# Attention and a channel MLP on one core: reordering the first batch's loads, casts and row work

## The chip, the core and the metric

The kernel runs on one core of a Trainium2 chip. The metric is device time in microseconds of one execution. Before the change it is 813.15 us, the median of five runs (812.42 to 814.14).

The engines named below: TensorE (PE in the profile, its weight loads PEld) multiplies matrices and writes to PSUM banks; VectorE (DVE) and ScalarE (ACT) do elementwise work and move PSUM results to SBUF; GpSimd (POOL) does some casts and issues the transfers that convert f32 to bf16 on the way; SyncE (SP) issues other transfers. Each engine runs its own instructions strictly in the order in which the program gives them, and waits at each for what it needs from the others.

## What is computed

Eight batches of 384 positions. First grouped attention: 16 query heads on 4 key and value heads, 64 wide. Its heads side by side are x, 384 x 1024. Then an MLP block in which tokens and channels are mixed in turn:

```python
scores = scale * np.matmul(q, k.transpose(0, 1, 3, 2))
attn = softmax(scores)                       # with the maximum taken off
x = np.matmul(attn, v)                       # heads side by side: B x 384 x 1024
a1 = alpha1 * x + beta1
tok = np.einsum('ts,bsd->btd', w_tok, a1)    # w_tok: 384 x 384
u = x + lam * tok
a2 = alpha2 * u + beta2
ch = np.maximum(a2 @ w_ch1, 0.0) @ w_ch2     # 1024 -> 4096 -> 1024
out = u + lam * ch
```

## The kernel before

**Stages.** `side(b)` lists the attention and the token mixing of batch b as small units; `main(b)` is the channel MLP of batch b, the bulk of TensorE's work. For b of 1 and more the units of `side(b)` are spread between the matmuls of `main(b - 1)`. Batch 0 has no MLP in front of it, so `side(0)` runs alone, and this is the stage that the change touches. Nothing reorders instructions: the order of the calls is the order on each engine.

**The order of the first batch.** There are 18 steps `scores(i)`, each with an exponential on ScalarE. After step i come the units that the table `at` lists for i (lines 375 to 382). The score tiles take turns in two PSUM buffers, so scores(i) needs the exponential of step i - 2. `av(p)` multiplies the weights of head pair p with v; its norm on VectorE is a reciprocal, a multiplication (into x) and a multiplication by a row (lines 242, 243, 247). `tok(p)` mixes tokens, and VectorE adds the result to x (line 266). `ut` transposes the result and ScalarE scales it (line 278). `k_transpose` and `q_transpose` turn k and q on TensorE and copy the result to kT and qT (lines 179, 190). The tags "tp" and "av" are one PSUM bank each and are shared by all transposes and row products, so each user of a tag waits until the last reader of the user before it is done.

**The rows alpha and beta.** The rows lie in a scratch of 32 partitions, `rows_f`, one block of 128 columns for each (0 alpha1, 1 beta1, 2 alpha2, 3 lam, 4 beta2). `scale_rows(i)` multiplies a row by lam (line 521). `split` cuts f32 rows into three bf16 parts, with a cast and a multiply and subtract (lines 529, 530), twice, and a last cast (533); on the way it uses the scratch `rows_t`. `spread` multiplies them out to all partitions on TensorE and copies the result to `vecs` (lines 325, 327), in two halves, `lower` and `upper`. `rows_r` makes the row R of w_tok's column sums times beta (lines 307 to 317); `fill_h` makes its counterpart H from beta's split (line 537). `tok` multiplies both (line 263). The scratches are all pieces of hT, which is free until the MLP starts:

```python
rows_f = hTf[:32, 9216:10496].bitcast(f32)
rows_t = hTf[:32, 10496:11520].bitcast(f32)
t = hTf[:32, 10496:10496 + S]          # in rows_r
```

**Loads.** SyncE's queue loads k (two tiles of two heads) and the rows; ScalarE's queue q's first group and v; GpSimd's queue the other three q groups (`load_q4`), w_tok, and the weights W1 (`load_w1`, chunks of 256 columns in a ring of five buffers), then the next batch's q and v and W2. v is cast to bf16 by GpSimd (line 545). `place_k` casts a k tile and doubles it, two instructions a call; the call `place_k(0, 1)`, heads 2 and 3, has both on GpSimd (line 101).

Of the kernel before, what the change touches and what calls it, by code (L numbers as in the profile page):

```python
# [12 lines left out]
def kernel(  # L13
# [21 lines left out]
    nc = tc.nc  # L35
# [7 lines left out]
    B, Hq, S, D = q.shape  # L43
# [23 lines left out]
    vt = [const.tile([P, NST, Hkv, D1], bf, tag=f"v{i}", name=f"v{i}") for i in range(2)]  # L67
# [25 lines left out]
    def place_k(b, i, hs=(0, 1)):  # L93
        if b not in k2s:
            k2s[b] = sb.tile([P, NST, Hkv, 2, D], bf, tag="k2", name="k2", bufs=1)
        copies = [nc.gpsimd.tensor_copy] * 2
        if b == 1 or b == 0 == i:
            copies = (nc.vector.tensor_copy, nc.vector.tensor_copy if i else nc.scalar.copy)
        lo, hi = hs[0], hs[-1] + 1
        for a in range(2):  # L100
            copies[a](out=k2s[b][:, :, 2 * i + lo:2 * i + hi, a, :], in_=ks[b][i][:, lo:hi].rearrange("p h st d -> p st h d"))
# [22 lines left out]
    def load_w1(n):  # L124
        if n < B * NCH:
            t = sb.tile([P, NDT, CW * P], bf, tag="w1", name="w1", bufs=RING)
            c = n % NCH
            nc.gpsimd.dma_start(out=t, in_=w1src[:, :, c * CW * P:(c + 1) * CW * P])  # L128
            w1_tiles[n] = t
# [28 lines left out]
    def side(b):  # L158
# [145 lines left out]
        def rows_r(tag):  # L304
            ps = psum.tile([P, 512], f32, tag=tag, name="r", bufs=1)
            for st in range(NST):
                nc.tensor.matmul(out=ps[:32, :S], lhsT=ones, rhs=wtokT[:, st, :], start=(st == 0),
                                 stop=(st == NST - 1))
            turned = ps[:, S:S + 2 * NP].rearrange("p (i n) -> p i n", i=2)
            for i, c in enumerate((2, 4)):  # L310
                nc.tensor.matmul(out=turned[:, i], lhsT=rows_f[:NP, c * P:(c + 1) * P], rhs=ident_f[:NP, :NP],
                                 is_transpose=True, start=True, stop=True, skip_group_check=True)
            t = hTf[:32, 10496:10496 + S]
            nc.vector.tensor_copy(out=t, in_=ps[:32, :S])
            nc.vector.scalar_tensor_tensor(out=R[:32], in0=t, scalar=masks[2], in1=ps[:32, :S], op0=MUL, op1=ADD)
            nc.vector.tensor_copy(out=al2T, in_=turned[:, 0])
            nc.vector.tensor_copy(out=a2T[:, :, S:S + 1], in_=turned[:, 1, :, None])
# [51 lines left out]
        lower, upper = range(NP // 2), range(NP // 2, NP)  # L369
        def av(p):  # L370
# [4 lines left out]
        at = {0: [(warmup, 3)], 1: [(k_transpose, 1, 1), (scale_rows, 0), (split, 0, 1, 0)],  # L375
              2: [(q_transpose, 2, 2, "av"), (split, 0, 1, 1)], 3: [(warmup, 1)],
              4: [(spread, lower, (0, 1), "tp"), (wtok_transpose, 0, "av")], 5: [(av, 0), (wtok_transpose, 1, "tp")],
              6: [(wtok_transpose, 2, "av"), (scale_rows, 1), (split, 1, 2), (k_transpose, 2)],
              7: [(av, 1), (q_transpose, 4, 2, "av")], 8: [(rows_r, "tp"), (fill_h, 0)],
              9: [(av, 2), (spread, upper, (0, 1), "av")], 10: [(q_transpose, 6, 2), (tok, 0)],  # L380
              11: [(av, 3)], 12: [(tok, 1), (ut, 0)], 13: [(av, 4), (tok, 2)], 14: [(ut, 1), (fill_h, 4), (tok, 3)],
              15: [(av, 5), (ut, 2)], 16: [(tok, 4), (ut, 3)], 17: [(av, 6), (tok, 5)]}
        for i in range(18):
# [70 lines left out]
    with tc.manual_schedule(engines=order):  # L454

        def warmup(n):
            warm = psum.tile([P, 512], f32, tag="mm", name="warm", bufs=2)
            for _ in range(n):
# [12 lines left out]
        qst, vst = (stage[:, i:i + Hkv * NST * D].rearrange("p (h st d) -> p h st d", h=Hkv, st=NST)  # L471
                    for i in (0, Hkv * NST * D))
# [28 lines left out]
        def load_q4(g):  # L501
            nc.gpsimd.dma_start(out=qgs[g], in_=q[0, g * G:(g + 1) * G].rearrange("h (p st) d -> p h st d", st=NST))
# [36 lines left out]
                                    in1=sel4[:, p:p + 4, None].to_broadcast([32, 4, P]), op=MUL)  # L539

        nc.gpsimd.dma_start(out=wtok_in, in_=moe_w_tok.rearrange("(p tt) s -> p tt s", tt=NST))
        load_q4(2)
        load_q4(3)
        place_k(0, 0, (0,))
        nc.gpsimd.tensor_copy(out=vt[0][:, :, :, :D], in_=vst.rearrange("p h st d -> p st h d"))
        load_w1(0)
        load_w1(1)
        place_k(0, 1)
        for c in range(2, RING):
            load_w1(c)  # L550

# [4 lines left out]
        for f in side(0):  # L556
            f()
        place_k(1, 0)
        place_k(1, 1)
        for b in range(B):  # L560
            us = side(b + 1) if b + 1 < B else []
            half = False
            done, t, loaded, flipped = 0, 0, b + 2 >= B, b + 2 >= B
            lead, span = (0.04, 0.82) if b == 0 else (0, 0.95)
            if not loaded:
                load_k(b + 2)
            for dt in main(b):
                t += dt
                half = not half
                if late and half:  # L570
                    late.pop(0)()
                if done < len(us) and done * t_all * span < len(us) * (t - t_all * lead):
                    us[done]()
                    done += 1
                if not loaded and t > t_all * 0.55:
                    loaded = True
                    place_k(b + 2, 0)
                    place_k(b + 2, 1)
                    load_q(b + 2)
                    load_v(b + 2)  # L580
                if not flipped and t > t_all * 0.85:
                    flipped = True
                    flip_k(b + 2)
                    flip_q(b + 2)
            while done < len(us):
                us[done]()
                done += 1
# [30 lines left out]
```

## Time and profile before

| | |
|---|---|
| median of five runs | 813.15 us |
| the profiled execution, its own time | 812.7 us |
| its span | 810.8 us |
| granted TensorE clock | 0.999 |
| TensorE busy | 795.9 us, 98% |
| VectorE, ScalarE, GpSimd busy | 345.2, 225.2, 176.1 us |
| first batch before its MLP | 0 to about 41 us |

The span runs from the first to the last instruction; the profiled execution took 1.9 us more than its span. In the timelines a row gives the start, the duration, the engine, the line, the operation, output<-input, the shape and the count of instructions; the bracket is the idle time of the engine ahead of it and what ended it. The chain of waits is the work that ended last, followed back. DMA rows on POOL give the time of issuing; landing comes later. In the first 41 us TensorE waits 1.32 us for the rows' split, 0.97 us for the copies of w_tok, 0.9 us for a copy of q, 0.63 us for an addition to x and 0.51 us for a copy of k, apart from its wait at the start.

### The profile page before, as it was taken

The numbers are of one execution on the slowest core, as the hardware profiler recorded it, in microseconds if no ns is written. First come the engines' busy times: TensorE is split into PE (matmuls) and PEld (weight loads), VectorE is DVE, ScalarE is ACT, GpSimd is POOL, SyncE is SP. The second block draws the span as 40 slices with busy tenths as digits, with TensorE's granted clock in tenths as the row PEclk, the third lists the DMA queues.
The fourth block names the chain that finished last, engine by engine and source line by source line (L and its number), as shares of the span: only waits on it lengthen the run. The fifth ranks groups of instructions, "written<-read, shape, count | busy, mean of one in ns | idle before, by whom it ended". The sixth has DMA issues, their size and how long they took to land.

```text
span 810.8 us, 14106 instructions
## 1 busy us (share of the span) xinstructions
PE 795.9 (98%) x6076; PEld 450.0 (56%) x6129; DVE 345.2 (43%) x671; ACT 225.2 (28%) x309; POOL 176.1 (22%) x230
## 2 busy tenths in 40 slices
PE   7999999999999999999999999999999999999997
PEld 4766555665556655566455654556555565556545
DVE  7745543244433444344452445434444344432122
ACT  5654311332113311233103331034211432102100
POOL 6135330234003230133202250022500321003000
PEclk9999999999999999999999999999999999999999
DMA  9999999999179992799848997499935999129611
GB/s 188 197 201 200 204 206 182 170 159 182 36 142 181 176 139 67 134 181 165 114 100 133 174 179 87 107 145 171 180 67 110 149 177 123 39 66 178 93 40 40
DMA packets 232494, 113.16 MB, mean 140 GB/s; under 512 B 81384, under 2 KB 226288, under 8 KB 232432
## 3 DMA queue, kind: packets, MB, share of 16 engines
q0 software_dynamic: 169152, 83.28, 83.2%
q1 hardware_dynamic: 62208, 28.20, 14.8%
q8 instruction: 48, 0.79, 0.4%
q10 hardware_dynamic: 1072, 0.79, 0.3%
q14 instruction: 14, 0.11, 0.0%
HBM read 170.53 MB, written 12.58 MB: 226 GB/s over the span
## 4 chain that ended last, share of the span: by engine, by line
PE 94%; DVE 4%; issue 1%; ACT 0%; DVEq 0%
PE ch L441 41%; PE h L407 39%; PE av L237 4%; PE sc L202 4%; PE tok L259 4%; DVE x L243 1%; DVE hT L417 1%; PE h L152 1%; DVE a1f L250 0%; DVE a L252 0%; PE warm L459 0%; PE ut L276 0%; DVE hT L530 0%; PE tp L188 0%; DVE hT L529 0%
## 5 line engine op out<-in xcount | busy, mean ns | idle before, releaser
L407 PE MATMUL h<-a2T,w 128*128 128x384 bf16 (+1 forms) x2016 | 349.5, 326 | 0.9 <-DVE hT L417 0.3
L441 PE MATMUL ch<-w,hT 128*128 128x512 bf16 (+2 forms) x1547 | 345.3, 370 | 4.3 <-issue 1.0
L407 PEld LDWEIGHTS <-w 128*128 128x128 bf16 x2016 | 189.4, 98 | 125.5 <-issue 8.7
L441 PEld LDWEIGHTS <-hT 128*128 128x128 bf16 x1600 | 146.3, 98 | 154.2 <-issue 5.8
L128 POOL DMA_DIRECT2D w<-in_moe_w_ch_dram x128 | 112.1, 876 | 538.9 <-PE h L407 495.3
L211 ACT ACTIVATE es<-sc 128x1024 bf16<-128x1024 f32 x126 | 123.3, 1021 | 289.5 <-PE sc L202 289.5
L417 DVE TENSOR_SCALAR hT<-h,bias 128x384 bf16<-128x384 f32 x128 | 79.1, 618 | 187.0 <-PE h L407 186.4
L415 ACT ACTIVATE hT<-h,bias 128x384 bf16<-128x384 f32 x128 | 74.2, 580 | 202.8 <-PE h L407 202.3
L446 DVE TENSOR_TENSOR o<-ch,vecs 128x512 f32<-128x512 f32 (+2 forms) x50 | 33.4, 667 | 91.1 <-PE ch L441 91.1
L266 DVE TENSOR_TENSOR x<-tok,x 128x384 f32<-128x384 f32 x64 | 35.5, 555 | 80.5 <-PE tok L259 78.2
L237 PEld LDWEIGHTS <-es 128*128 128x128 bf16 x1008 | 45.8, 97 | 20.5
L237 PE MATMUL av<-v,es 128*128 128x65 bf16 x1008 | 49.0, 193 | 0.0
L202 PE MATMUL sc<-qT,kT 64*128 64x384 bf16 (+2 forms) x576 | 45.7, 273 | 1.2 <-DVE qT L190 0.9
L259 PEld LDWEIGHTS <-wtokT 128*128 128x128 bf16 x576 | 37.9, 98 | 12.8 <-issue 1.0
L242 DVE RECIPROCAL rinv<-av 128x6 f32<-128x6 f32 x64 | 12.3, 192 | 70.5 <-PE av L237 70.4
L259 PE MATMUL tok<-a,wtokT 128*128 128x128 bf16 x504 | 37.3, 219 | 0.0
L243 DVE TENSOR_TENSOR x<-av,rinv 128x384 f32<-128x384 f32 x64 | 35.7, 558 | 2.2
L202 PEld LDWEIGHTS <-kT 64*128 64x128 bf16 x576 | 19.9, 94 | 29.2 <-issue 23.9
L447 DVE TENSOR_TENSOR o<-o,x 128x512 f32<-128x512 f32 (+2 forms) x50 | 33.6, 671 | 1.7
L270 DVE TENSOR_TENSOR a<-x,vecs 128x384 bf16<-128x384 f32 x56 | 31.8, 567 | 1.9
L252 DVE TENSOR_TENSOR a<-a1f,vecs 128x384 bf16<-128x384 f32 x56 | 31.2, 558 | 2.2
L250 DVE TENSOR_TENSOR a1f<-x,vecs 128x384 f32<-128x384 f32 x56 | 31.2, 558 | 1.9
(76 smaller groups left out, 195.1 us busy)
## 6 DMA issues: line engine op xcount, KB each, us to landing
w<-in_moe_w_ch_dram POOLq DMA_DIRECT2D x138, 512.0 KB, 7.9
out_dram<-o SPq DMA_DIRECT2D x47, 256.0 KB, 2.1
q_raw<-in_q_dram POOLq DMA_DIRECT2D x28, 192.0 KB, 7.0
kst<-in_k_dram SPq DMA_DIRECT2D x16, 192.0 KB, 4.0
w<-in_moe_w_ch_dram POOLq DMA_DIRECT2D x1, 2048.0 KB, 15.3
v<-in_v_dram POOLq DMA_DIRECT2D x21, 64.0 KB, 6.9
w<-in_moe_w_ch_dram POOLq DMA_DIRECT2D x4, 256.0 KB, 8.8
a2T<-a SPq DMA_TRANSPOSE x54, 2.3
```

The source lines that it names most:

```text
L128: nc.gpsimd.dma_start(out=t, in_=w1src[:, :, c * CW * P:(c + 1) * CW * P])
L202: nc.tensor.matmul(out=sc[:, hh, k % 4:k % 4 + n], lhsT=kT[r, sk, 2 * p // G, :], rhs=qT[r, p, st:st + n, :], start=True, stop=True)
L211: nc.scalar.activation(out=e, in_=sc, func=EXP, scale=scale_qk)
L237: nc.tensor.matmul(out=av[:, hh, sq, :], lhsT=ess[k // 4][:, m % 2, k % 4, :], rhs=vb[:, sk, hk, :], start=(sk == 0), stop=(sk == NST - 1))
L243: nc.vector.tensor_tensor(out=x[:, :, cols(p)].rearrange("p st (h d) -> p h st d", h=2), in0=av[:, :, :, :D], in1=rinv.to_broadcast([P, 2, ...
L259: nc.tensor.matmul(out=ps[:, tt, :], lhsT=wtokT[:, st, tt * P:(tt + 1) * P], rhs=a1s[p][:, st, :], start=(st == 0), stop=(st == NST - 1 an ...
L266: nc.vector.tensor_tensor(out=u, in0=ps, in1=u, op=ADD)
L407: nc.tensor.matmul(out=ps[:, :n], lhsT=w1[:, dt, j * P:(j + 1) * P], rhs=a2T[:, dt, :n], start=(dt == 0), stop=(dt == NDT - 1))
L415: nc.scalar.activation(out=hT[:, nt, :], in_=ps[:, :S], func=RELU, bias=c1)
L417: nc.vector.tensor_scalar(out=hT[:, nt, :], in0=ps[:, :S], scalar1=c1, scalar2=0.0, op0=ADD, op1=mybir.AluOpType.max)
L441: nc.tensor.matmul(out=ps[:, lo:hi], lhsT=hT[:, nt, ms * P:(ms + 1) * P], rhs=w2[:, nt, dw * 512 + lo:dw * 512 + hi], start=(nt == 0), sto ...
L447: nc.vector.tensor_tensor(out=o[:, lo:hi], in0=o[:, lo:hi], in1=x[:, ms, c], op=ADD)
```

## The change

Four things in the first batch. On GpSimd, the loads of q groups 2 and 3 are issued behind v's cast rather than ahead of it, and `place_k(0, 1)` stands ahead of W1's first two chunks rather than behind them. In the table `at`, the scaling and the split of beta move from step 6, ahead of the copy of k, to step 7, behind the norm of pair 1 and the copy of q. The cast at the start of `rows_r` (line 314) and the copy of the upper half of alpha's spread (line 327) go from VectorE to ScalarE. TensorE's order of instructions is the same.

```diff
-            nc.vector.tensor_copy(out=t, in_=ps[:32, :S])
+            nc.scalar.copy(out=t, in_=ps[:32, :S])
             nc.vector.scalar_tensor_tensor(out=R[:32], in0=t, scalar=masks[2], in1=ps[:32, :S], op0=MUL, op1=ADD)
...
-              6: [(wtok_transpose, 2, "av"), (scale_rows, 1), (split, 1, 2), (k_transpose, 2)],
-              7: [(av, 1), (q_transpose, 4, 2, "av")], 8: [(rows_r, "tp"), (fill_h, 0)],
-              9: [(av, 2), (spread, upper, (0, 1), "av")], 10: [(q_transpose, 6, 2), (tok, 0)],
+              6: [(wtok_transpose, 2, "av"), (k_transpose, 2)],
+              7: [(av, 1), (q_transpose, 4, 2, "av"), (scale_rows, 1), (split, 1, 2)], 8: [(rows_r, "tp"), (fill_h, 0)],
+              9: [(av, 2), (spread, upper, (0, 1), "av", "ACT")], 10: [(q_transpose, 6, 2), (tok, 0)],
...
         nc.gpsimd.dma_start(out=wtok_in, in_=moe_w_tok.rearrange("(p tt) s -> p tt s", tt=NST))
+        place_k(0, 0, (0,))
+        nc.gpsimd.tensor_copy(out=vt[0][:, :, :, :D], in_=vst.rearrange("p h st d -> p st h d"))
         load_q4(2)
         load_q4(3)
-        place_k(0, 0, (0,))
-        nc.gpsimd.tensor_copy(out=vt[0][:, :, :, :D], in_=vst.rearrange("p h st d -> p st h d"))
+        place_k(0, 1)
         load_w1(0)
         load_w1(1)
-        place_k(0, 1)
         for c in range(2, RING):
             load_w1(c)
```

`place_k(0, 0, (0,))` runs on VectorE and ScalarE and keeps its place there.

## The prediction

> **What bounds the kernel now.** I read the page first, then the chain of waits, then the timeline of each engine up to 45 us, because every line of the diff acts on the first batch.
>
> ```profile
> span 810.8 us, 14106 instructions
> PE 795.9 (98%) x6076; PEld 450.0 (56%) x6129; DVE 345.2 (43%) x671; ACT 225.2 (28%) x309; POOL 176.1 (22%) x230
> PE 94%; DVE 4%; issue 1%; ACT 0%; DVEq 0%
> ```
>
> TensorE carries 94% of the chain. The 4% on VectorE is where a change can act, and most of it lies between 8 and 24 us. TensorE's instructions there, with what ended each wait:
>
> ```profile
> 11.79 0.38 PE L325 MATMUL vec<-hT,stage 128*128 128x128 bf16 x4 [1.32 <-DVE hT L533]
> ...
> 15.05 0.49 PE L177 MATMUL tp<-ident,k 128*128 128x128 bf16 x6 [0.97 <-DVE wtokT L300]
> 15.81 0.72 PE L237 MATMUL av<-v,hT 128*128 128x65 bf16 x18
> 16.36 0.50 PE L188 MATMUL tp<-ident,qg 128*128 128x128 bf16 x6
> ...
> 17.69 0.65 PE L307 MATMUL r<-wtokT,stage 128*32 128x384 bf16 x3 [0.51 <-DVE kT L179]
> 19.45 0.39 PE L202 MATMUL sc<-qT,kT 64*128 64x384 bf16 x4 [0.90 <-DVE qT L190]
> 20.99 0.51 PE L188 MATMUL tp<-ident,qg 128*128 128x128 bf16 x6
> 24.11 0.33 PE L259 MATMUL tok<-hT,wtokT 128*128 128x128 bf16 x3 [0.63 <-DVE x L266]
> ```
>
> Each stall ends on VectorE. The chain from 12.66 (av of pair 0) to 24.11 is one VectorE instruction behind another, without a gap from 13.35; from 24.11 to 40.9 it is TensorE alone. So the first batch ends as much earlier or later as tok(1) does, which stands at 24.11 and waits for the add of tok(0), L266, at 23.51. The main part after it is TensorE at 98% and moves along.
>
> VectorE and GpSimd, around the places that move:
>
> ```profile
> 9.92 0.68 DVE L529 CAST hT<-hT 32x128 bf16<-32x128 f32 x1
> 10.63 0.65 DVE L530 SCALAR_TENSOR_TENSOR hT<-hT,stage 32x128 f32<-32x128 bf16 x1
> 11.32 0.41 DVE L533 CAST hT<-hT 32x128 bf16<-32x128 f32 x1
> ...
> 15.18 0.27 DVE L521 TENSOR_TENSOR hT<-hT 32x128 f32<-32x128 f32 x1
> 16.21 0.34 DVE L529 CAST hT<-hT 32x128 bf16<-32x128 f32 x1
> 16.59 0.34 DVE L530 SCALAR_TENSOR_TENSOR hT<-hT,stage 32x128 f32<-32x128 bf16 x1
> 17.10 0.54 DVE L179 COPY kT<-tp 128x768 bf16<-128x768 bf16 x1
> 19.31 0.54 DVE L314 CAST hT<-r 32x384 bf16<-32x384 f32 x1
> ```
>
> ```profile
> 9.70 0.82 POOL L545 CAST v<-stage 128x768 bf16<-128x768 f32 x1 [4.92 <-DMA stage<-in_v_dram]
> 10.47 1.77 POOL L128 DMA_DIRECT2D w<-in_moe_w_ch_dram  x2
> 12.22 0.97 POOL L101 CAST k<-kst 128x384 bf16<-128x384 f32 x2
> ```
>
> The reader is to see that the same three split instructions take 0.68, 0.65 and 0.41 beside GpSimd's cast and issues, and 0.34, 0.34 and 0.33 at 16.21; and that GpSimd idles 4.92 us before v's cast.
>
> **Part 1, beta's split and the two copies: VectorE's queue, step by step.** Pitches are start to start, as the timeline has them.
> - Beta's scale and split took 15.18 to 17.10, 1.92. In their place kT's copy comes first. It needs the k transposes (15.05 + 0.49 = 15.54), so it starts at 15.57: 0.39 idle instead of work at 15.18.
> - kT's pitch is 0.47, so VectorE is free at 16.04. The norm of pair 1 waits for its av, which TensorE starts at 15.81 as before; pair 0's norm began 0.75 after its av (12.60 to 13.35). So 16.56: another 0.52 idle.
> - The norm's three instructions, 0.21, 0.59 and 0.48, lead to qT's copy at 17.84, pitch 0.46; then beta's 1.92 from 18.30 to 20.22.
> - L314 goes to ScalarE, saving VectorE the 0.57 between 19.31 and 19.88. But its target is columns 10496 on of hT, and the split's scratch rows_t begins at the same column: t covers 384 bf16 columns, and beta's part of rows_t is the 256 from 10752. So L314 must wait for the split's second L530, which reads that scratch: it starts at 17.84 + 0.46 + 0.30 + 0.35 + 0.38 + 0.38 = 19.71 and ends 20.05. ScalarE is free at 18.30 and waits, with the exponential of scores 9 queued behind it. The copy's price is ScalarE's cast of 128x384 from the same kind of tile, 0.48 (5.73); so L314 runs 20.08 to 20.56, and VectorE's L315 starts at 20.60 instead of 20.22: 0.38 of new wait.
> - L327's upper copy goes to ScalarE: VectorE saves the pitch 0.60 (22.44 to 23.04).
> - Sum to the add of tok(0): -0.57 - 0.60 + 0.39 + 0.52 + 0.38 = **+0.12 us**. It starts at 23.63, not 23.51, and tok(1) at 24.23.
>
> What waits behind: the exponential of scores 9 ran 19.95 and now 20.56; L327 at 21.54 (ScalarE's row for this copy is 0.585); then exponentials 10 to 12 at 22.10, 23.08, 24.06 (were 21.16, 22.59, 23.57). Scores 12 need number 10 done, at 23.12; TensorE comes there at 23.51, so ScalarE's lateness is covered by 0.39, and after exponential 12 ends at 25.08 the next step, ut(0), comes at 25.42. On TensorE, q's last transposes (20.99) now wait for L317, the last reader of their bank, until 21.42, where the row showed no wait; the three waits at 17.69, 19.45 and 24.11 shrink or vanish instead. TensorE's order itself is unchanged. Bounds of this part: if L314 had no wait -0.26; if ScalarE's cast took as long as its widest copy, 0.585, +0.23.
>
> **Part 2, GpSimd.** Its casts and issues follow each other without a gap once v has landed: cast 9.70 to 10.47; two q issues of 1.50 together (at 3.29 before) to 11.97; k's two casts, 0.97, to 12.94 (ended 13.19); W1's first two, 1.77, and the next three, 2.63, to 17.34 (ended 15.73). So W1 chunk 0 is issued 2.5 later, at 12.9, and everything behind on this queue 1.6 later.
> - k's casts: wanted at 15.05, ready 12.9. SP's second load of the next batch's k waits on them and goes 0.2 earlier. Nothing.
> - W1: chunk 0 landed 16.3 and the fifth 28.6; wanted at 33.0 and after 41. Chunk 5 is issued at 41.66 when its buffer comes free and landed after 6.3, at 48.0; with the queue 1.6 behind 49.6, wanted at about 51.6. Hidden, with 2 us in hand.
> - q groups 2 and 3: issued at 10.47 and 11.2. Group 1 took 5.0 to land with an empty queue ahead, groups 2 and 3 took 8.3 and 9.1 behind wtok, which landed at 9.3. By the first row group 2 is there at 15.5, by the second at 18.8. TensorE wants it at 16.36; VectorE's copy of it stands at 17.84, so up to 17.3 it costs nothing. I take 5 to 6, since wtok and v are gone by then: nothing.
> [...]
> - v's cast: v's last packets share the queues with q groups 2 and 3 only from about 8 us, so it lands between 9.70 and about an us sooner. What this is worth is how the cast meets alpha's split. That split's second step took 9.92 to 11.73, 1.81, and beta's 16.21 to 17.29, 1.08: the meeting cost 0.73, and TensorE waited for it (1.32 at 11.79). An earlier cast meets the split's first step instead; and the k casts, two of 0.52, come 1.5 after it, into the second step. So from -0.73 (both miss) to +0.93 (0.73 x 1.04 / 0.82, k's casts are met too). I take 0, the row of v landing as it did.
> [...]
>
> **The sum.** +0.12 against the profiled execution's 812.7 (span 810.8 and 1.9 around it), which lies 0.45 under the median 813.15 of the five. Against that median: **813.3 us**, no change that can be told: 0.2%, 1.6 us, is about what a measurement of this kernel can tell from none.
>
> **Rivals.**
> - *Slower: q group 2 comes late.* Every us after 17.3 delays VectorE's whole queue and the end by as much. At 18.8 (its old 8.3): +1.5 + 0.1, 814.8; at 19.6 (the 9.1): +2.4, 815.6. It passes 1.6 from a landing 8.3 us after the issue. For it: its old rows. Against: those had wtok ahead of them.
> - *Faster: the clash goes.* v lands before 7.8, its cast falls into VectorE's idle 1.36 us before 8.36, and k's casts miss: -0.73 + 0.12, 812.5. Were the whole wait of 1.32 at 11.79 to go and L314 to wait for nothing, 813.15 - 1.32 - 0.26 = 811.6, the most that the rows give. Against: v's wait ended at 9.70, and k's second half landed at 10.1, so its casts can't come before.
> - *The change moves nothing:* v lands at 9.70 all the same and the ScalarE copies wait for VectorE. This is nearly my forecast.
> - *W1 starves TensorE:* needs over 3.6 us of delay at chunk 5; 1.6 is in sight. Each us more would cost one.
>
> **How the numbers follow.** Forecast, with the clash 0.5 either way: 0.55. The clash gone or worse, still within 1.6: 0.17. q late or W1 late beyond it: 0.16. The most of the gains together, or something that no row shows: 0.12. So within 0.2%: 0.72, slower 0.16, faster 0.12. The range runs from TensorE's wait at 11.79 gone altogether (-1.32 + 0.12) to q at its old 8.3: 811.9 to 814.8.
>
> **What would show it.** Right: ScalarE's L314 starting at about 20.1 after idling since 18.3; kT's copy at 15.6; q's last transposes waiting for L317; tok(1) at 24.2 +- 0.7; q group 2 landed by 17. Wrong: L314 at 18.3; v's cast before 8; split instructions under 0.4 at 9.9 to 11.8; a TensorE wait on a qg load at 16.4, or on W1 near 51.

## The result and the profile after

The changed kernel takes 814.37 us, the median of 21 runs (812.86 to 817.07), beside 812.72 us for the kernel before (39 runs, 811.10 to 814.14). The ratio is 1.0022, with a 95% interval of 1.0015 to 1.0028. So the forecast of 813.3 us was 1.1 us short and its range (811.9 to 814.8) holds the time. But the loss lies just outside the 0.2% that I called the least that can be told, on the side to which I gave a chance of 0.16; and it turned out that my sum had not seen where it arises. That the range reaches the measured time is luck: its upper end stands for q group 2 landing late, which did not happen.

The page of after, first the span, the engines and the chain of waits:

```profile
span 811.5 us, 14108 instructions
...
PE 797.6 (98%) x6076; PEld 451.1 (56%) x6129; DVE 344.0 (42%) x669; ACT 226.0 (28%) x311; POOL 176.5 (22%) x230
...
PE 94%; DVE 4%; issue 1%; ACT 0%; DVEq 0%; ACTq 0%
```

The profiled execution took 813.3 us (span 811.5); before's took 812.7. It is one of the quicker executions of this kernel, 1.1 us under its median, so what it shows is not the whole loss. TensorE's waits between 8 and 27 us in its timeline:

```profile
10.96 0.38 PE L325 MATMUL vec<-hT,stage 128*128 128x128 bf16 x4 [1.23 <-DVE hT L533]
...
14.74 0.80 PE L177 MATMUL tp<-ident,k 128*128 128x128 bf16 x6 [0.45 <-DVE wtokT L300]
...
22.10 0.49 PE L188 MATMUL tp<-ident,qg 128*128 128x128 bf16 x6 [1.32 <-DVE a2T L317]
...
24.80 0.33 PE L259 MATMUL tok<-hT,wtokT 128*128 128x128 bf16 x3 [0.23 <-DVE x L266]
```

Compared with before: the wait for alpha's split is 1.23 instead of 1.32, q's last transposes wait 1.32 for L317 where they had not waited, and tok(1) starts at 24.80 instead of 24.11. The span grew by 0.7, as tok(1) did. VectorE, and then ScalarE, in the same execution:

```profile
9.43 0.90 DVE L530 SCALAR_TENSOR_TENSOR hT<-hT,stage 32x128 f32<-32x128 bf16 x1
10.36 0.55 DVE L533 CAST hT<-hT 32x128 bf16<-32x128 f32 x1
...
15.58 0.56 DVE L179 COPY kT<-tp 128x768 bf16<-128x768 bf16 x1 [0.62 <-PE tp L177]
...
20.25 0.34 DVE L530 SCALAR_TENSOR_TENSOR hT<-hT,stage 32x128 f32<-32x128 bf16 x1
...
21.18 0.60 DVE L315 SCALAR_TENSOR_TENSOR stage<-hT,stage,r 32x384 bf16<-32x384 bf16 x1 [0.34 <-ACT hT L314]
```

```profile
20.68 0.47 ACT L314 CAST hT<-r 32x384 bf16<-32x384 f32 x1 [1.19 <-DVE hT L530]
21.05 1.01 ACT L211 ACTIVATE hT<-sc 128x1024 bf16<-128x1024 f32 x1
```

Four things stand here as I had them: in alpha's split L530 is slow beside v's cast (0.90), and so is L533 right behind it (0.55); kT's copy starts at 15.58 (said: 15.57) after waiting for the k transposes; L314 has moved to ScalarE and waits for the split's last L530, because both use the same columns of hT; and VectorE's L315 waits 0.34 for L314 (said: 0.38). GpSimd in the same execution:

```profile
9.37 0.82 POOL L543 CAST v<-stage 128x768 bf16<-128x768 f32 x1 [6.07 <-DMA stage<-in_v_dram]
10.14 1.49 POOL L502 DMA_DIRECT2D qg<-in_q_dram  x2
11.62 0.97 POOL L101 CAST k<-kst 128x384 bf16<-128x384 f32 x2
12.53 4.39 POOL L128 DMA_DIRECT2D w<-in_moe_w_ch_dram  x5
```

v's cast ran at 9.37 (before 9.70), and q groups 2 and 3 landed 3.8 and 4.5 us after they were issued, so the first rival, q late, did not happen. What I had not looked at is what the transfers do meanwhile. Busy time in three stretches, the last three columns being TensorE's granted clock, the mean share of the DMA engines (their packets' time added up, so it can pass 1) and GB/s; first before, then after:

```profile
10.00:11.50 1.50, 0.39 (x4) 0.21 (x4) 1.43 (x3) 1.50 (x3) 1.50 (x3) 1.00 1.18 212
11.50:14.00 2.50, 2.21 (x39) 1.56 (x39) 1.81 (x5) 1.47 (x3) 2.50 (x5) 1.00 0.92 105
14.00:20.00 6.00, 3.62 (x56) 2.24 (x54) 5.69 (x17) 3.03 (x4) 4.73 (x7) 1.00 1.38 201
```

```profile
10.00:11.50 1.50, 0.54 (x9) 0.44 (x10) 0.99 (x3) 1.12 (x2) 1.50 (x3) 1.00 0.00 0
11.50:14.00 2.50, 2.50 (x33) 1.63 (x33) 1.73 (x5) 1.05 (x2) 2.50 (x5) 0.53 1.22 134
14.00:20.00 6.00, 5.55 (x66) 3.51 (x65) 4.12 (x12) 3.04 (x3) 5.70 (x8) 0.63 1.36 194
```

Two things are new. Between 10.0 and 11.5 us the DMA engines moved 212 GB/s before and nothing after: q groups 2 and 3 filled that time before, and now nothing moves until GpSimd has done v's cast and issued them. And TensorE's clock was at half from about 11.7 to 18.5 us in this execution (0.50 granted from 12 to 18, 1.00 up to 11.5 and again from 18.5).

### The profile page after: what moved, and what is told of

It reads as the page before. It is cut to its first block, busy times and chain, and to the rows that moved or that the text cites. A ratio compares the mean times of both kernels' runs of the same rounds, so it can differ in the third digit from the quotient of the medians.

```text
span 811.5 us, 14108 instructions
## 1 busy us (share of the span) xinstructions
PE 797.6 (98%) x6076; PEld 451.1 (56%) x6129; DVE 344.0 (42%) x669; ACT 226.0 (28%) x311; POOL 176.5 (22%) x230
## 4 chain that ended last, share of the span: by engine, by line
PE 94%; DVE 4%; issue 1%; ACT 0%; DVEq 0%; ACTq 0%
PE ch L441 41%; PE h L407 39%; PE av L237 4%; PE sc L202 4%; PE tok L259 4%; DVE x L243 1%; DVE hT L417 1%; PE h L152 1%; DVE a1f L250 0%; DVE a L252 0%; PE warm L459 0%; PE ut L276 0%; DVE hT L530 0%; DVE rinv L242 0%; PE tp L177 0%
```

## Experiments

Every run below was timed in five rounds against the kernel before on the same chip. The table puts together what the later text uses; each profiled execution is a single one. "tok(1)" is where it starts, "q's transpose" is the transfer that turns batch 2's q (`flip_q`, line 117 of before), its start and its time on SyncE's queue, and the last two columns are TensorE's waits for that transpose and for a chunk of W1.

| run | ratio, 95% interval | tok(1) | q's transpose | wait for it | wait for W1 |
|---|---|---|---|---|---|
| before | 1 | 24.11 | 131.33, 4.33 | none | none |
| after | 1.0022 (1.0015 to 1.0028) | 24.80 | 133.81, 4.18 | none | none |
| after_again | 1.0018 (1.0006 to 1.0030) | 23.06 | 134.42, 4.01 | 0.96 | 0.86 |
| after_own_t | 1.0032 (1.0020 to 1.0045) | 23.20 | 136.46, 3.70 | 3.53 | 0.22 |
| only_rows | 0.9999 (0.9991 to 1.0008) | 25.11 | 132.01, 4.26 | none | none |
| only_pool | 1.0014 (1.0005 to 1.0022) | 24.28 | 135.06, 4.02 | 1.42 | none |
| q_behind | 1.0047 (1.0029 to 1.0066) | 22.73 | 134.46, 4.03 | 1.31 | 0.96 |
| before_more_bytes | 1.0026 (1.0011 to 1.0040) | 24.63 | 134.51, 4.12 | 0.69 | none |
| after_less_bytes | 1.0004 (0.9996 to 1.0013) | 24.71 | 130.91, 4.11 | none | none |
| after_q2_early | 1.0020 (1.0007 to 1.0033) | 23.63 | 130.06, 7.39 | 1.18 | none |
| before_q2_early | 0.9993 (0.9985 to 1.0002) | 22.72 | 129.12, 5.30 | none | none |
| after_hold | 1.0040 (1.0025 to 1.0056) | 23.46 | 130.96, 7.22 | 2.00 | none |
| before_hold | 1.0019 (1.0010 to 1.0027) | 25.29 | 131.87, 7.72 | 1.57 | none |
| after_hold2 | 1.0017 (1.0005 to 1.0029) | 24.34 | 129.47, 3.69 | none | 0.96 and 0.34 |

### Waits of the row work, or the clock?

From the trace of after I had two theories. Wait theory: the 0.7 us are VectorE's and TensorE's new waits around L314, L315 and L317. Clock theory: they come from TensorE's half clock in the first batch. Four kernels went together: the changed kernel once more; the changed kernel with a scratch of its own for L314; GpSimd's part of the change alone; everything but GpSimd's part.

The changed kernel again, without an edit:

> The changed kernel itself, beside the kernel before on the same chip. All theories: 1.0015 to 1.0028 of before. The clock theory (TensorE falls to half clock when it idles about 1 us twice, at 10 to 11 us and before q's last transposes) expects the granted clock to fall to 0.5 for a few us between 8 and 25 us in this profile too. The wait theory (L314 on ScalarE waits for beta's split, and TensorE's q transposes wait for what follows) expects L314 near 20.1 to 20.7 and the q transposes near 21.4 to 22.1, at full clock or not.

Measured: 814.05 against 812.76 us, 1.0018. The granted clock was 1.00 throughout the first batch, so the clock theory falls as the cause of a loss that is there without it. Nor does the drop come with the change: six of the 14 profiled executions, with a mean granted clock of 0.995 to 0.998, have one in the first batch, three of them with before's code there (before_more_bytes, before_q2_early, before_hold). And among the executions whose granted clock was 1.000 the loss is still there: a median of 813.57 us in after_again (5 executions) against 812.4 for the kernel before on the same chip (6). And tok(1) started at 23.06, a full microsecond earlier than in before. So in this execution the first batch was quicker and the kernel still slower. Two waits appear later, on TensorE, that the trace of before does not have (the timeline of TensorE):

```profile
51.57 0.83 PE L407 MATMUL h<-a2T,w 128*128 128x385 bf16 x4 [0.86 <-DMA w<-in_moe_w_ch_dram]
...
139.90 0.61 PE L202 MATMUL sc<-qT,kT 64*128 64x384 bf16 x8 [0.96 <-DMA qT<-q_raw]
```

The changed kernel with another scratch:

```diff
-            t = hTf[:32, 10496:10496 + S]
+            t = hTf[:32, 7296:7296 + S]
```

> The changed kernel, with the copy of line 314 writing to columns of hT that nothing else uses, so that ScalarE no longer waits for the split's scratch. Wait theory: L314 runs right behind the exponential at about 18.3 to 19.5, L315 loses its 0.34 to 0.38 us of wait, and the time falls by 0.3 to 0.5 us against the changed kernel. Clock theory: no more than that, as TensorE still idles before q's last transposes, which wait for L317 behind the split. GpSimd theory (the loss comes from the new order on GpSimd's queue): no change of the time.

Measured: 815.32 us, 1.0032. L314 started at 17.77 without a wait, and L315 did not wait for it, so it was the shared columns that made it wait. q's last transposes waited 0.86 for L317 instead of 1.29 to 1.32, as the wait theory wants, yet the kernel was not faster; its scores waited 3.53 us for batch 2's q. The wait theory falls too.

GpSimd's part alone (the last block of the diff shown with the change, on the kernel before):

> The kernel before with GpSimd's new order alone. GpSimd theory: most of the loss, +1.0 to +1.7 us. Wait theory: within 0.4 us of before. Clock theory: slower only if the granted clock falls below 1.0 somewhere in the first 30 us; else within 0.4 us.

Measured: 814.00 us, 1.0014.

The change without GpSimd's part (GpSimd's order as before, the rest as after):

> The changed kernel with GpSimd's old order: beta's split moved and the two copies on ScalarE. Wait theory: most of the loss, +1.0 to +1.7 us, from the split standing between qT's copy and L315 to L317. GpSimd theory: within 0.4 us of before. By the prediction's own sum it is +0.1.

Measured: 813.09 us, 0.9999. So the row work and the ScalarE copies are worth nothing that can be told, and GpSimd's order carries the loss, which shows at 140 us and not in the first batch. The pair of rows that matters is SyncE's queue in before:

```profile
127.02 3.30 SPq L113 DMA_TRANSPOSE kT<-k  x1
131.33 4.33 SPq L117 DMA_TRANSPOSE qT<-q_raw  x1
```

with TensorE's scores that read it, which do not wait,

```profile
138.88 0.61 PE L202 MATMUL sc<-qT,kT 64*128 64x384 bf16 x8
```

and in only_pool, with TensorE's row that waits for it:

```profile
127.26 3.27 SPq L113 DMA_TRANSPOSE kT<-k  x1
135.06 4.02 SPq L117 DMA_TRANSPOSE qT<-q_raw  x1
```

```profile
140.57 0.61 PE L202 MATMUL sc<-qT,kT 64*128 64x384 bf16 x8 [1.42 <-DMA qT<-q_raw]
```

q's transpose cannot start before q's last group has landed. In before that was at 131.2 (issued at 113.36, 17.8 us to land), 0.9 after k's transpose was out of the queue; in only_pool at 134.9 (116.43 and 18.5), 4.4 after. In after_again, after_own_t and only_pool, where they wait, the scores start 5.48 to 5.51 us after the transpose does. So before, with its transpose at 131.33, could have started them at 136.8 and did at 138.88: 2.0 us in hand. After's profiled execution, with its scores at 139.63, had 0.3 in hand:

```profile
127.74 3.38 SPq L113 DMA_TRANSPOSE kT<-k  x1
133.81 4.18 SPq L117 DMA_TRANSPOSE qT<-q_raw  x1
```

The traces also show that in these executions nothing else adds to the time. Where no load is waited for on the way, these scores start 114.8 us after tok(1). From the scores to the end of the span it is 671.9 us in eleven of the 14 profiled executions, before, after, after_again and only_pool among them; it is 1.6 to 1.7 more in after_own_t and after_hold, which fall to half clock behind their wait, and in after_hold2, which waits for W1 there. So the start of these scores decides the time. In only_pool they start 1.69 us later than in before, for a wait of 1.42 and a tok(1) that is 0.17 later, and the span is 1.7 us longer. In after the 0.7 us are tok(1) alone.

### Stream theory

So a third theory: GpSimd's loads form one stream that the DMA engines serve without a pause from about 13 to 131 us at some 200 GB/s: W1, batch 1's q and v, W2, W1 again, batch 2's q and v. Nothing in it can make up for a gap. The page of before has the DMA engines' busy tenths in slices of 20.3 us, 9 in each of the first ten:

```profile
DMA  9999999999179992799848997499935999129611
```

In stretches of 4 to 10 us they move 188 to 208 GB/s from 14 to 132 us, and nothing from 138 to 140, where the stream has drained. The change puts a gap of 1.5 us at its head, and everything in the stream lands that much later or more, up to batch 2's q, whose slack was 2.0 us. I called the rival the first-batch theory: the loss is made before 25 us and the wait at 140 us only takes the place of another.

512 KB of W2 loaded twice in the kernel before, first batch untouched:

```diff
         load_w2(0, 0, 2)
+        load_w2(1, 0, 8)
```

> The kernel before, with 512 KB of W2 loaded twice: once more, right behind the first W2 load, which no one waits for. Nothing before 30 us moves; the stream behind is 2.6 us later (512 KB at 199 GB/s). Stream theory: chunk 5 of W1 is wanted 2 us after it lands, so a wait of 0 to 0.9 us near 51 us, and a wait of 0.6 to 3 us of batch 2's first scores on q's transpose; ratio 1.0010 to 1.0040. First-batch theory: the first batch is untouched, the stream has room, ratio 0.9993 to 1.0007.

Measured: 814.42 us, 1.0026. The wait is there, with the first batch's code as in before:

```profile
140.15 0.61 PE L202 MATMUL sc<-qT,kT 64*128 64x384 bf16 x8 [0.69 <-DMA qT<-q_raw]
```

512 KB less in the changed kernel:

```diff
-        load_w2(0, 0, 2)
+        for i in range(3):
+            load_w2(0, i, 8)
+        nc.gpsimd.memset(w2[:, 12:16, 0:512], 0.0)
```

> The changed kernel with 512 KB less in the stream: rows 12 to 15 of the first half of W2 are not loaded but set to zero by GpSimd where it is idle near 35 us, so a part of the second product is left out of the output and no instruction of TensorE. The mirror of the run that loaded 512 KB twice: the first batch as changed, the stream 2.6 us earlier from 31 us on. Stream theory: no wait for W1 near 51 us, none of batch 2's scores for q's transpose (q's last group near 131 to 132), few executions above 815 us; ratio 0.9988 to 1.0006. First-batch theory: 1.0014 to 1.0025, as for the change.

Measured: 812.76 us, 1.0004, and no wait for a load. The slowest of its 11 runs took 813.86; 6 of the changed kernel's 21 took over 815. q's last group landed at 129.6 (in after at 133.7), and SyncE's queue has q's transpose right behind k's:

```profile
127.60 3.11 SPq L113 DMA_TRANSPOSE kT<-k  x1
130.91 4.11 SPq L117 DMA_TRANSPOSE qT<-q_raw  x1
```

These two runs decide for the stream. Bytes added behind the old first batch cost about what the change costs (0.26% with an interval of 0.11 to 0.40, beside 0.22%); bytes taken away behind the new one give it back.

One half of GpSimd's change alone, q's groups behind v's cast, k's copies where they were:

```diff
-        load_q4(2)
-        load_q4(3)
         place_k(0, 0, (0,))
         nc.gpsimd.tensor_copy(out=vt[0][:, :, :, :D], in_=vst.rearrange("p h st d -> p st h d"))
+        load_q4(2)
+        load_q4(3)
```

> The kernel before with only q's groups 2 and 3 issued behind v's cast; k's copies stay behind W1's first two chunks. Stream theory: the DMA engines stand still for about 1 us of 10 to 11.5 us, and W1 starts 0.6 to 0.9 earlier than with k's copies ahead of it, so about half of the lag: q's last group of batch 2 lands 0.7 to 1.5 us later than before's 131.2, wait of the scores 0 to 0.8, ratio 1.0002 to 1.0012. First-batch theory: q's lateness itself is not felt, ratio 0.9993 to 1.0003.

Measured: 815.63 us (7 runs), 1.0047: a miss. I had it at half of the loss, and it is more than the whole. The transpose starts at 134.46, so q's groups alone are enough to make the stream late. Its TensorE was early (tok(1) at 22.73) and ran into both waits, 0.96 for W1 and 1.31 for q. Why that should cost 3 us at the median is not shown: its profiled execution is its fastest, 813.82. Half clock has a part in it: its two slowest executions, 818.22 and 819.85, have the lowest granted clocks of the seven, 0.995 and 0.994.

### Can the loads be put in an order that hides it?

Batch 2's k copies, q and v ahead of the five W1 chunks of batch 1 (2.5 MB):

```diff
-                if not loaded and t > t_all * 0.55:
+                if not loaded and t > t_all * (0.55 if b else 0.45):
```

> The changed kernel, with batch 2's k copies, q loads and v loads put ahead of the five W1 chunks of batch 1 on GpSimd (2.5 MB, some 12 us of the stream). Stream theory: GpSimd's loads run without a pause from 13 to 131 us, the change starts them later, and this is paid where batch 2's first scores wait for q's transpose (1.0 to 3.5 us in runs so far); with q's last group landing some 10 us earlier (near 122 instead of 134) the wait is gone, and the loss of 0.22% falls to 0.00 to 0.10%, what is left being the wait for W1 near 51 us, up to 0.9. First-batch theory: the loss is made before 25 us and q's late landing only hides in it; the ratio stays at 1.0015 to 1.0025.

> The kernel before with the same move of batch 2's loads. In its profile q's transpose was 2.0 us ahead of the scores that read it, so both theories expect a ratio of 0.9985 to 1.0005; below 0.9993 it would say that some executions of the kernel before also wait there. Something else is learned: whether the five W1 chunks of batch 1, now 5 us later, are missed near 141 us; they landed near 110 to 120, so no wait for them is expected.

Measured: 1.0020 for the changed kernel, 0.9993 for the kernel before. The first is a miss. q landed in time and its transpose started at 130.06, but it then took 7.39 us instead of about 4, which I put down to the last of the five W1 chunks, since these now stood behind q (when they landed is not shown), and TensorE waited 1.18:

```profile
126.58 3.29 SPq L113 DMA_TRANSPOSE kT<-k  x1
130.06 7.39 SPq L117 DMA_TRANSPOSE qT<-q_raw  x1
```

```profile
139.64 0.61 PE L202 MATMUL sc<-qT,kT 64*128 64x384 bf16 x8 [1.18 <-DMA qT<-q_raw]
```

Next, two of those five chunks (1 MB) were to be held back until batch 1 runs, and 512 KB of W2 moved behind chunk 5 of W1, in both kernels. `load_w1` with a second argument makes tiles for three chunks and issues the third ahead of the other two, since I took it that the third would have to wait for a buffer:

```diff
             if b == 0 and c == NCH - RING:
-                for i in (6, 7):
+                for i in (3, 6, 7):
...
             if b == 0 and c == NCH - 1:
-                for i in range(RING):
+                for i in range(RING - 2):
...
-            if b or c + RING < NCH:
+            if (b, c) == (1, 0):
+                load_w1(NCH + RING - 2, 1)
+            elif b or c + RING < NCH:
...
-        load_w2(0, 0, 2)
+        for i in range(3):
+            load_w2(0, i, 8)
```

> The changed kernel, everything computed, with loads put in another order: rows 12 to 15 of W2's first half go from the first W2 load to the group issued near 73 us (the stream is 2.6 us earlier at W1's chunk 5), and two of the five W1 chunks of batch 1 that are loaded ahead (1 MB) are issued after the first product of batch 1 has given its buffer back, near 142 us, behind the chunk that takes that buffer; so 1 MB less stands between q's last group of batch 2 and q's transpose and beside it. Stream theory: q's last group lands some 5 us earlier, q's transpose follows k's at once near 131 us, no waits; ratio 0.9985 to 1.0006. First-batch theory: 1.0014 to 1.0025. Above 1.003 it would be the held chunks that come late: wanted near 151 us, issued near 143.

> The same new order of loads in the kernel before. Its profile has no wait for a load behind 25 us, so by the profile nothing is to be gained: 0.9992 to 1.0005. Stream theory adds that executions in which the stream runs late (those above 813 us) are cut: 0.9985 to 1.0000. Against the run of the changed kernel with this order it shows what the change is worth where the stream is out of the way: my sum says 0.1 us, so the two within 0.1% of each other.

Measured: 1.0040 and 1.0019, both misses, and both profiles show the wait of the run before, 2.00 and 1.57 us. The chunks were not held: the ring had two free buffers, so they left at 123 to 126 us, ahead of q's transpose, which took 7.22 and 7.72 us. In after_hold:

```profile
130.96 7.22 SPq L117 DMA_TRANSPOSE qT<-q_raw  x1
```

Neither profile has a wait for W1 near 51 us, which the move of 512 KB was to prevent. Then with a hold that holds: the two loads stand behind a copy on GpSimd that needs batch 0's last output. The moves of W2 stay, and `load_w1` has no second argument again.

```diff
+                if (b, dw, ms) == (0, NDW - 1, NST - 1):
+                    nc.gpsimd.tensor_copy(out=held, in_=o[:, :1])
+                    for i in (RING - 2, RING - 1):
+                        load_w1(NCH + i)
```

> The changed kernel with the order of loads of the two runs before, but with the hold made real: the two W1 chunks (1 MB) stand behind a GpSimd copy of one column of batch 0's last output, which is there near 137 us; in those runs the framework gave them free buffers and they left at 123 to 126, beside q's transpose, which took 7.2 to 7.7 us instead of 4.0. Stream theory: q's last group lands near 127 to 128, q's transpose follows k's at once, takes about 4 us with nothing beside it, and its reader does not wait; the held chunks are issued near 138, land by 147 and are wanted near 148.5. Ratio 0.9988 to 1.0006. If the loss were not the transpose's lateness, the ratio stays at 1.0015 to 1.0045 as with the change and the two runs before; if the held chunks come late, TensorE waits for W1 near 148 and the ratio is above 1.001.

Measured: 814.20 us, 1.0017, a miss again, by the late chunks that I had named as the other case. The transpose did what the theory says: at once behind k's, 3.69 us, no wait.

```profile
127.25 2.04 SPq L114 DMA_TRANSPOSE kT<-k  x1
129.47 3.69 SPq L118 DMA_TRANSPOSE qT<-q_raw  x1
```

But the hold ended at 140.0 instead of 137, the DMA engines stood still from 136 to 140 us, and the chunks came late by 0.96 and 0.34 us:

```profile
136.00:140.00 4.00, 4.00 (x27) 1.85 (x26) 1.38 (x2) 0.40 (x1) 0.00 (x0) 1.00 0.00 0
```

```profile
148.59 5.48 PE L408 MATMUL h<-a2T,w 128*128 128x384 bf16 x32 [0.96 <-DMA w<-in_moe_w_ch_dram]
...
154.68 2.77 PE L408 MATMUL h<-a2T,w 128*128 128x384 bf16 x16 [0.34 <-DMA w<-in_moe_w_ch_dram]
```

So none of the three orders rids the changed kernel of waiting: in two of them the same scores wait, because the transpose itself takes longer, and in the third W1's readers wait. No order tried makes the change pay, and none of these kernels beats the kernel before by more than can be told; before_q2_early at 0.9993 comes nearest.

## Why the prediction was right, and where it was not

- **The row work, +0.12 us.** only_rows, 0.9999 with an interval of 0.9991 to 1.0008, agrees. The single terms (-0.57, -0.60, +0.39, +0.52, +0.38) are too small to be tested one by one: tok(1) started anywhere from 22.7 to 25.3 us over the 14 profiled executions, and at 22.72, 24.11, 24.63 and 25.29 in the four with before's code for that stage. The waits that I derived from the code (kT's copy for the k transposes, L314 for the split's scratch, q's transposes for L317) are all in the trace.
- **v's cast against the split, taken as 0.** In after's execution the clash stayed: 1.23 us of wait instead of 1.32. In after_again v came later (cast at 10.43), the split's second step ran ahead of the cast in 0.20, 0.34 and 0.21, and the wait was 0.33. But in the four executions with before's code the same wait lies anywhere from 0.33 to 1.88, so what it is goes with the execution, not with the change. L530 at 10.63 began 0.11 us after the cast's end and still took 0.65. And one reading in the working was off: beta's quick split at 16.21 stood beside GpSimd's issues too (batch 1's q loads, 15.73 to 18.73), so issues alone do not make these instructions slow; what does is not shown.
- **k's casts, "Nothing".** They were ready in time in after's execution. In after_again, with v late, TensorE waited 1.27 us for them; in three executions with the old place of `place_k(0, 1)` it waited 1.51.
- **q groups 2 and 3.** They landed after 3.8 and 4.5 us; I took 5 to 6. They were not late, and the slower rival's mechanism did not occur.
- **"Everything behind on this queue 1.6 later", "Hidden, with 2 us in hand".** This is the step that failed. In after's profiled execution chunk 5 landed at 49.55, where I had put it, 49.6. In after_again, after_own_t, only_pool and q_behind it landed at 51.05 to 51.73, 3.1 to 3.8 later than before's 47.96, and in the three of them in which TensorE was early it was waited for, 0.22 to 0.96 us. So the rival that I let go with "needs over 3.6 us; 1.6 is in sight" does occur, and with it a sign that I had listed for being wrong, a wait on W1 near 51. And I followed the delay to one reader only, W1's chunk 5. The next readers of the same stream were batch 2's q and its transpose, 2.0 us ahead of the scores at 138.88, and that slack stood in the trace of before: SyncE's rows at 127.02 and 131.33, TensorE's at 138.88, DMA busy in tenths at 9 in every slice to 203 us.
- **The sum.** I wrote +0.12 for the whole. The loss is 1.65 us between the medians; GpSimd's order, at 0, was the term that was mis-sized, and alone it measures +0.14% (0.05 to 0.22%), 1.1 us.

What stays open: each kernel was profiled in one execution, so how the loss of the others divides between W1's chunk, batch 2's q and the clock (below) is not shown. Why the lag of the stream is 1.6 us in one execution and over 3 in others is not settled either. The record shows only that it is there by 40 us: until then the DMA engines moved 192 GB/s on the mean in before, 184 in after, and 178 to 181 in after_again, after_own_t, only_pool and q_behind, and only_pool and q_behind lost a part of it behind the gap, with 176 to 191 GB/s from 14 to 30 us (before 196 to 201). So in these two the lag is more than the gap, and a steady 200 GB/s is too simple a picture. Why q_behind is slower than both halves together was not settled.

## What to carry to other kernels

When a change delays a queue of loads, ask first whether the DMA engines behind it are ever idle afterwards. If they are not, the delay is not hidden by the first reader with slack: follow the stream until it drains, and compare the delay with the smallest slack of all its readers, and look at what else is in the queues by then: batch 2's q transpose took 7.2 to 7.7 us instead of about 4 in three runs with W1 chunks loaded right behind q. Here a gap early in a full stream was paid at the readers with the least in hand, at two of them in after_again, and none of the orders tried hid it; that no order could is not shown.

## What the runs showed of the hardware

**Batch 2's q transpose took nearly twice as long in three runs with W1 chunks right behind q's loads.** It took 3.69 to 4.33 us in ten of the 14 profiled executions, 5.30 in before_q2_early, 7.39 in after_q2_early, 7.22 in after_hold and 7.72 in before_hold. In these four, W1 chunks of 512 KB follow batch 2's q and v in GpSimd's order; in after_hold two of them were issued at 123.40 and 124.81 us, in before_hold at 124.35 and 126.30. In after_hold2, where the next chunks were issued from 140.53 on, behind the transpose's end, it took 3.69. How the DMA engines divide their time between such loads and the transpose is not shown.

**After waits of 2.0 and 3.5 us TensorE ran at half clock for 3.4 us.** In after_own_t TensorE waited 3.53 us until 141.96 for q's transpose, and from about 143.4 to 146.8 its granted clock was 0.50. The stretches' columns are as above, the third from the right being the clock:

```profile
140.00:141.00 1.00, 0.00 (x0) 0.00 (x0) 0.00 (x0) 0.00 (x0) 0.00 (x0) 1.00 1.14 217
...
143.00:144.00 1.00, 1.00 (x7) 0.53 (x5) 0.00 (x0) 1.00 (x3) 0.00 (x0) 0.68 0.98 317
144.00:145.00 1.00, 1.00 (x5) 0.49 (x4) 0.00 (x0) 0.86 (x1) 0.00 (x0) 0.50 0.23 75
145.00:146.00 1.00, 1.00 (x5) 0.49 (x4) 0.22 (x1) 0.00 (x0) 0.00 (x0) 0.50 0.06 16
146.00:147.00 1.00, 1.00 (x6) 0.44 (x5) 0.40 (x1) 0.00 (x0) 0.89 (x1) 0.62 0.00 0
```

At half clock these 3.4 us lose 1.7 us of work, half of the wait itself, and from the scores to the end this execution is 1.6 us longer than before. after_hold, with a wait of 2.00, shows the same half clock from about 141.6 to 145.0; the waits of 0.69 to 1.57 at that place left it at 1.00. In the first batch of after, a wait of 1.23 was followed by half clock from about 11.7 to 18.5 us, 6.8 us; before's wait of 1.32 at the same place left it at 1.00, and so did after's other wait of 1.32, until 22.10, so a wait of that length does not settle it. What sets a drop off, and what sets its length, is not shown.
